# Output projection: the last four rows of every head loaded by four DMA engines, the other rows by sixteen

## The chip, the cores and the metric

One core of one Trainium2 chip runs the program. The metric is the time on the device in microseconds. The profile has its own measure, the span from the first to the last instruction; the time is 1.7 to 2.1 us longer than the span, and that difference will matter.

## The reference, cut to what matters

```python
g = sigmoid((x * gate_w).sum(-1))
q = (x @ wq) as 32 heads of 128              # x is one row of 576
a = softmax(q k^T / sqrt(128)) v, last 4096 keys, 16 kv heads
a = concat(heads) @ wo                       # wo: 4096 x 576, row 128*h + d
b = gelu(x @ w1 + b1) @ w2 + b2              # 576 -> 4608 -> 576
out = g * a + (1 - g) * b
```

All tensors are bf16. With one row of x, every weight and every cached key and value is read once and used once: 53.6 MB in all.

## The kernel before

The large loads are issued in order by SyncE; each covers 128 partitions. The output projection `wo` and the second half of `w2` are the last five of them. The weights `wo` lie as 32 consecutive rows per partition, so partition 4h+a holds rows 32a to 32a+31 of head h. The attention output is spread over partitions in the same way by one small product (`om` with `lo32b`), and every row then costs two products into `y_ps`.

```python
    # ... loads of w1, wq, K; scores; softmax ...
    v_t = [load("v_t", "CD"[g], A_v_cache, g) for g in range(2)]
    nc.sync.dma_start(out=w2_t[:, 0:NJ, :], in_=w2_src[:, 0])
    v_t.append(load("v_t", "A", A_v_cache, 2))
    # ...
    v_t.append(load("v_t", "C", A_v_cache, 3))
    # ...
    RO = Hq * Dh // P                                   # 32
    wo_src = A_wo.rearrange("(p r) n -> p r n", r=RO)
    for r0, r1 in ((0, 16), (16, RO)):
        nc.sync.dma_start(out=wo_t[:, r0:r1, :], in_=wo_src[:, r0:r1, :])
    for j0, j1 in ((0, 10), (10, 16), (16, 18)):
        nc.sync.dma_start(out=w2_t[:, NJ + j0 : NJ + j1, :], in_=w2_src[:, 1, j0:j1, :])
    # om = attention output x (g / sum), one column block per stripe a
    ov_mm = nc.tensor.matmul(ov_ps[:], lhsT=om..., rhs=lo32b[:], start=True, stop=True)
    nc.vector.tensor_copy(out=ov[:], in_=ov_ps[:])
    late = [(gt, f, w2_t[:, f, :]) for f in range(6, NJ)]
    # ... then wo rows and w2 rows in order of arrival; each one two matmuls into y_ps
```

Of the kernel before, what the change touches and what calls it, by code (L numbers as in the profile page):

```python
# [9 lines left out]
FP32 = mybir.dt.float32  # L10
BF16 = mybir.dt.bfloat16
I32 = mybir.dt.int32
ACT = mybir.ActivationFunctionType
ALU = mybir.AluOpType
# [4 lines left out]
def kernel(  # L19
# [15 lines left out]
    nc = tc.nc  # L35

    P = 128
    D = 576
    Hq, Hkv, Dh = 32, 16, 128
# [10 lines left out]
    NI = 2 * D // P  # L50
# [15 lines left out]
        main.instructions.insert(at, first)  # L66

    nc.at_finalize(first_load_ahead)

    def keep_weights(nc):  # L70
        body = nc.main_func.blocks[1]
        loaded, kept = None, []
        for i in body.instructions:
            if type(i).__name__ == "InstLdweights":
                w = i.ins[0]
                key = (w.memref, w.offset, tuple(w.ap), i.tile_size, i.tile_position)
                sync = i.sync_info
                free = sync is None or not (sync.on_wait or sync.on_update)
                if key == loaded and free:
                    continue  # L80
                loaded = key
            elif type(i).__name__ == "InstMatmult" and i.ldweights is not False:
                loaded = None
            kept.append(i)
        body.instructions = kept
# [58 lines left out]
    const = ctx.enter_context(tc.tile_pool(name="const", bufs=1))  # L144
# [4 lines left out]
    ps_m = ctx.enter_context(tc.tile_pool(name="ps_m", bufs=2, space=bass.MemoryType.PSUM))  # L149
# [24 lines left out]

    one_b = const.tile([1, 2], BF16, name="one_b")
    nc.gpsimd.memset(one_b[:], 1.0)
    NCC = 2 * NI + 32 + 4 + 16 + P
    low = const.tile([P, NCC], I32, name="low")
    mask = const.tile([P, NCC], I32, name="mask")
    c0 = 0  # L180
    for base, pattern, keep in (
        (0, [[1, NI], [1, 2]], 1),
        (128, [[-1, 32]], 31),
        (128, [[-32, 4]], 96),
        (128, [[-8, 16]], 120),
        (128, [[-1, P]], 7),
    ):
        n = 1
        for step, num in pattern:
            n *= num  # L190
        nc.gpsimd.iota(low[:, c0 : c0 + n], pattern=pattern, base=base, channel_multiplier=1)
        nc.gpsimd.memset(mask[:, c0 : c0 + n], keep)
        c0 += n
    nc.vector.tensor_tensor(out=low[:], in0=low[:], in1=mask[:], op=ALU.bitwise_and)
    is0 = const.tile([P, NCC], FP32, name="is0")
    nc.gpsimd.tensor_scalar(
        out=is0[:], in0=low[:], scalar1=0.0, scalar2=None, op0=ALU.is_equal
    )
    alt = is0[:, 0 : 2 * NI].rearrange("p (i t) -> p i t", t=2)
    lo32 = is0[:, 2 * NI : 2 * NI + 32]  # L200
    hi4 = is0[:, 2 * NI + 32 : 2 * NI + 36]
    ones = const.tile([P, P], FP32, name="ones")
    nc.gpsimd.memset(ones[:], 1.0)
    ident = const.tile([P, P], BF16, name="ident")
# [4 lines left out]
        out=perm[:],  # L209
        in_=perm[:],  # L210
        pattern=[[-64, 2], [-1, 2], [0, 4], [-2, 32]],
        compare_op=ALU.not_equal,
        fill=1.0,
        base=0,
        channel_multiplier=1,
    )
    lo32b = const.tile([P, 32], BF16, name="lo32b")
    nc.gpsimd.tensor_copy(out=lo32b[:], in_=lo32)
    c0 = 2 * NI + 36
    hi16 = const.tile([P, 16], FP32, name="hi16")  # L220
    nc.gpsimd.tensor_scalar(
        out=hi16[:], in0=is0[:, c0 : c0 + 16], scalar1=-SCALE, scalar2=None, op0=ALU.mult
    )
    same8 = is0[:, c0 + 16 : NCC]
    row_of = const.tile([HB, 16, HB, 2], BF16, name="row_of")
    nc.gpsimd.memset(row_of[:], 0.0)
    nc.gpsimd.affine_select(
        out=row_of[:],
        in_=row_of[:],
        pattern=[[0, 16], [-1, HB], [0, 2]],  # L230
        compare_op=ALU.not_equal,
        fill=1.0,
        base=0,
        channel_multiplier=1,
# [4 lines left out]
        out=foreign[:],  # L239
        in_=foreign[:],  # L240
        pattern=[[0, P], [-1, HB]],
        compare_op=ALU.not_equal,
        fill=0.0,
        base=0,
        channel_multiplier=1,
# [4 lines left out]
        out=xdup.rearrange("p (d t) -> p d t", t=2),  # L250
        in_=x_row.rearrange("p (d o) -> p d o", o=1).to_broadcast([1, D, 2]),
    )
    xs_ps = ps_m.tile([P, NI, 1], FP32, name="xs_ps", tag="m")
    for i in range(NI):
        nc.tensor.matmul(  # L255
            xs_ps[:, i, :],
            lhsT=xdup[:, i : 2 * D : NI],
            rhs=one_b[0:1, 0:1],
            start=(i == 0),
            stop=(i == NI - 1),  # L260
# [4 lines left out]
        out=x2[:], in0=xs_ps[:].to_broadcast([P, NI, 2]), in1=alt, op=ALU.mult  # L265
# [5 lines left out]
        out=junk_row,  # L271
        in0=x_row,
        in1=gw_row,
        scale=1.0,
        scalar=0.0,
        op0=ALU.mult,
# [8 lines left out]
    g_t = const.tile([P, 1], FP32, name="g_t")  # L285
# [3 lines left out]
        out=omg[:], in0=g_t[:], scalar1=-1.0, scalar2=1.0, op0=ALU.mult, op1=ALU.add  # L289
# [2 lines left out]
    nc.vector.tensor_scalar(  # L292
        out=b2g[:], in0=b2_row, scalar1=omg[0:1, 0:1], scalar2=None, op0=ALU.mult
    )
    gh = const.tile([P, 1, 4], FP32, name="gh")
    nc.vector.tensor_scalar(
        out=gh[:, 0, :], in0=hi4, scalar1=g_t[:, 0:1], scalar2=None, op0=ALU.mult
    )


# [19 lines left out]
    for j in range(NJ):  # L320
        nc.tensor.matmul(
            h_ps[:, j:NF:NJ],
            lhsT=b1_t[:, j:FH:NJ],
            rhs=ident[0:2, 0:2],
            start=(j == 0),
            stop=False,
# [5 lines left out]
    for i in range(NI):  # L332
        for j in range(NJ):
            nc.tensor.matmul(  # L334
                h_ps[:, j:NF:NJ],
                lhsT=w1_t[:, i, j:FH:NJ],
                rhs=x2[:, i, :],
                start=False,
                stop=(i == NI - 1 and j == NJ - 1),
# [9 lines left out]
        out=poly[:],  # L349
        in0=z2[:],  # L350
        scalar1=2.0 * C0 * 0.044715,
        scalar2=2.0 * C0,
        op0=ALU.mult,
# [11 lines left out]
        out=gt[:], in0=hacc[:], scalar=omg[:, 0:1], in1=r_t[:], op0=ALU.mult, op1=ALU.mult  # L365
# [4 lines left out]
    for i in range(NI):  # L370
        for j in range(Hq // 2):
            nc.tensor.matmul(  # L372
                q_ps[:, j : Hq : Hq // 2],
                lhsT=wq_t[:, i, j * Dh : (j + 1) * Dh],
                rhs=x2[:, i, :],
                start=(i == 0 and j == 0),
                stop=(i == NI - 1 and j == Hq // 2 - 1),
# [5 lines left out]
    for j in range(4):  # L383
        nc.tensor.matmul(
            qj_ps[:, j, :, :].rearrange("p g q -> p (g q)"),
            lhsT=perm[:, j, :, :].rearrange("p b l -> p (b l)"),
            rhs=q_b[:],
            start=True,
            stop=True,
        )  # L390
    for b in range(4):
# [6 lines left out]
            out=diag[:, :, :, 0:8],  # L398
            in_=qj_ps[quad].rearrange("p j g q -> p g j q"),
# [17 lines left out]
    def queue(engine, emit):  # L417
        if engine in issued:
            with tc.issue_after(issued[engine].ins):
                issued[engine] = emit()  # L420
        else:
            issued[engine] = emit()

    def load(name, tag, cache, g):
        tile_ = big.tile([P, NCK, Dh], BF16, name=name, tag=tag)
        src = cache[0, HB * g : HB * g + HB, Sk - W : Sk, :].rearrange(
            "b (k c) d -> k b (c d)", k=NKP
        )
        nc.sync.dma_start(out=tile_[:].rearrange("p c d -> p (c d)"), in_=src)
        return tile_  # L430
# [105 lines left out]
    v_t = [load("v_t", "CD"[g], A_v_cache, g) for g in range(2)]  # L536
    nc.sync.dma_start(out=w2_t[:, 0:NJ, :], in_=w2_src[:, 0])
    v_t.append(load("v_t", "A", A_v_cache, 2))
    o_ps = ps_m.tile([P, Hq, 1], FP32, name="o_ps", tag="m")

    def value_products(g):
        for c in range(NCK):
# [16 lines left out]
        out=ls[:],  # L559
        in0=same8[:, 0:8].rearrange("p (o q) -> p o q", o=1).to_broadcast([P, NG, 8]),  # L560
        in1=sums[:].to_broadcast([P, NG, 8]),
        op=ALU.mult,
# [6 lines left out]
            t_ps, lhsT=ones[:], rhs=ls[:].rearrange("p g q -> p (g q)"), start=True, stop=True  # L569
        ),  # L570
    )
    rg = const.tile([P, Hq, 1], FP32, name="rg")
# [2 lines left out]
    nc.vector.tensor_tensor(  # L575
        out=rgh[:],
        in0=rg[:].to_broadcast([P, Hq, 4]),
        in1=gh[:].to_broadcast([P, Hq, 4]),
        op=ALU.mult,
    )  # L580
    queue("pe", lambda: value_products(3))


    RO = Hq * Dh // P
    wo_t = big.tile([P, RO, D], BF16, name="wo_t", tag="D")
    wo_src = A_wo.rearrange("(p r) n -> p r n", r=RO)
    for r0, r1 in ((0, 16), (16, RO)):
        nc.sync.dma_start(out=wo_t[:, r0:r1, :], in_=wo_src[:, r0:r1, :])  # L588
    for j0, j1 in ((0, 10), (10, 16), (16, 18)):
        nc.sync.dma_start(out=w2_t[:, NJ + j0 : NJ + j1, :], in_=w2_src[:, 1, j0:j1, :])  # L590

    om = const.tile([P, Hq, 4], BF16, name="om")
    nc.vector.tensor_tensor(  # L593
        out=om[:], in0=o_ps[:].to_broadcast([P, Hq, 4]), in1=rgh[:], op=ALU.mult
    )
    with tc.issue_after(issued["pe"].ins):
        for f in range(6):
            y_add(gt[:, f : f + 1], w2_t[:, f, :])
    ov_ps = ps_m.tile([P, RO], FP32, name="ov_ps", tag="m")
    ov_mm = nc.tensor.matmul(  # L600
        ov_ps[:], lhsT=om[:].rearrange("p h a -> p (h a)"), rhs=lo32b[:], start=True, stop=True
    )
    ov = const.tile([P, RO], BF16, name="ov")
    nc.vector.tensor_copy(out=ov[:], in_=ov_ps[:])

    late = [(gt, f, w2_t[:, f, :]) for f in range(6, NJ)]
    wo_at = [(ov, r, wo_t[:, r, :]) for r in range(RO)]
    w2_at = [(gt, f, w2_t[:, f, :]) for f in range(NJ, NF)]
    late += wo_at[0:8] + wo_at[16:RO] + wo_at[8:13] + w2_at[0:10] + wo_at[13:16] + w2_at[10:]
    before = ov_mm  # L610
    for n, (vec, at, row) in enumerate(late):
# [37 lines left out]
```

## Time and profile before

| | before |
|---|---|
| time, median of 6 runs | 132.50 us (132.35 to 132.66) |
| span of the profiled run | 130.7 us |
| loads' queue, share of 16 DMA engines | 96.4% |
| TensorE busy | 61% |

The main lines of the page stand in the prediction. How to read them: the share of the loads' queue says that the DMA engines are busy nearly all the time, so the kernel is bound by moving bytes, and a product counts only where a landing waits for it. The last pieces of the chain that ended last, in order of time (start, duration, what), show it again:

```profile
93.23 34.61 DMA w_t<-in_B_w_dram
127.84 0.04 issue
127.89 1.19 PE y_ps L306 x16
129.07 0.43 DVE out_row L617
```

The load named here is issued at 93 us and lands at 127.84; for 34.61 us it only stands behind others. What follows its landing takes 1.6 us plus the store.

One thing is not on the page: a load is done when the slowest of its sixteen engines is. The trace stores sixteen increments of the load's semaphore, one for each of the sixteen chains of packets that the prediction describes, and the load counts as landed with the last. For the last piece of w2 in the kernel before, in us of the span:

```
126.66 126.67 126.88 126.90 126.99 127.04 127.07 127.09
128.13 128.20 128.29 128.33 128.35 128.43 128.49 128.58
```

Eight engines finish before the other eight, on average by 1.44 us.

### The profile page before, as it was taken

Reading aid. Unit: us, or ns where it says so; the run is one execution under the profiler, and the core shown is the slowest. Engines: PE = TensorE matmul, PEld = TensorE weight load, DVE = VectorE, ACT = ScalarE, POOL = GpSimd, SP = SyncE. Lnnn points to the kernel's source line nnn. Section 1 sums busy time; section 2 is a strip of 40 time slices with the busy share of each in tenths; the row PEclk is TensorE's granted clock in tenths of the full one; section 3 lists DMA queues with packets and bytes.
Section 4 is the critical chain, followed back from the end, with each engine's and each line's share of the span. In section 5 each row is a group of like instructions: output and inputs, shape, how many; then the busy total and the mean of one; then the engine's idle time right before and its main releaser. Section 6 shows DMA issues by size and latency. Waiting matters only on the chain.

```text
span 130.7 us, 2382 instructions
## 1 busy us (share of the span) xinstructions
PE 79.9 (61%) x1138; PEld 46.0 (35%) x1071; DVE 51.9 (40%) x47; ACT 8.1 (6%) x17; POOL 8.2 (6%) x28
## 2 busy tenths in 40 slices
PE   0037999466002998859909986987100930999573
PEld 0037949366000121211201121677000920945441
DVE  0053000400069969999999995604000010010001
ACT  3000000002100000030003003020000000000001
POOL 6029600000000000000000000000000000000000
PEclk9999999999999999999995999965555555556999
DMA  7999999899899999999999999999989999999980
GB/s 220 431 442 423 474 422 474 372 451 466 381 426 471 401 411 471 411 411 471 421 411 451 441 401 441 413 417 458 456 381 441 461 386 407 434 422 422 398 330 24
DMA packets 2468, 53.75 MB, mean 411 GB/s; under 512 B 278, under 2 KB 282, under 8 KB 540
## 3 DMA queue, kind: packets, MB, share of 16 engines
q1 hardware_dynamic: 2450, 53.61, 96.4%
q8 instruction: 8, 0.13, 0.4%
q10 hardware_dynamic: 10, 0.01, 0.0%
HBM read 53.62 MB, written 0.00 MB: 410 GB/s over the span
## 4 chain that ended last, share of the span: by engine, by line
DMA 54%; DVE 24%; PE 13%; issue 6%; SPq 1%; DVEq 0%
DMA k_t<-in_A_k_cache_dram 27%; DMA w_t<-in_B_w_dram 26%; DVE kt L441 19%; PE s_ps L463 7%; PE o_ps L543 5%; DVE m L479 3%; DVE pt L512 2%; PE y_ps L306 1%; SPq L588 1%; DVE mr L482 1%; PE mt_ps L488 0%; DVE out_row L617 0%; SPq L172 0%; SPq L590 0%; SPq L168 0%
## 5 line engine op out<-in xcount | busy, mean ns | idle before, releaser
L463 PE MATMUL s_ps<-kt,qz_flat 128*128 128x512 bf16 x128 | 32.3, 409 | 17.3 <-DVE kt L441 10.4
L441 DVE STREAM_TRANSPOSE kt<-k_t 128x4096 f32<-128x4096 f32 x8 | 35.3, 4432 | 11.8 <-DMA k_t<-in_A_k_cache_dram 10.7
L543 PE MATMUL o_ps<-pt,v_t 128*128 128x8 bf16 x512 | 14.2, 167 | 16.7 <-DMA v_t<-in_A_v_cache_dram 15.4
L463 PEld LDWEIGHTS <-qz_flat 128*128 128x128 bf16 x64 | 6.8, 106 | 40.1 <-issue 40.0
L543 PEld LDWEIGHTS <-v_t 128*128 128x128 bf16 x512 | 14.1, 103 | 17.5 <-DMA v_t<-in_A_v_cache_dram 15.6
L334 PE MATMUL h_ps<-x,w_t 128*128 128x2 bf16 x162 | 10.4, 202 | 0.0
L334 PEld LDWEIGHTS <-w_t 128*128 128x128 bf16 x162 | 10.2, 162 | 0.5 <-issue 0.4
L306 PE MATMUL y_ps<-w_t,gt 128*1 128x288 bf16 x72 | 7.4, 361 | 1.1 <-DMA w_t<-in_B_w_dram 1.1
L500 ACT ACTIVATE p_t<-s_ps,negm 128x1024 bf16<-128x1024 f32 x4 | 4.5, 1114 | 50.6 <-DVE negm L496 50.6
L573 DVE RECIPROCAL rg<-mt_ps 128x32 f32<-128x32 f32 x1 | 0.4, 358 | 15.8 <-PE mt_ps L568 15.8
L512 DVE STREAM_TRANSPOSE pt<-p_t 128x1024 bf16<-128x1024 bf16 x4 | 4.9, 1224 | 2.7 <-ACT p_t L500 2.7
L372 PE MATMUL q_ps<-x,wq_t 128*128 128x2 bf16 x144 | 4.0, 166 | 3.1 <-DMA wq_t<-in_A_wq_dram 3.1
L306 PE MATMUL y_ps<-wo_t,ov 128*1 128x288 bf16 x64 | 4.9, 299 | 1.4 <-DMA wo_t<-in_A_wo_dram 1.4
L343 DVE COPY hacc<-h_ps 128x36 f32<-128x36 f32 x1 | 0.2, 196 | 13.2 <-PE h_ps L334 13.2
L617 DVE CAST out_row<-y_ps 1x288 bf16<-1x288 f32 x1 | 0.4, 445 | 12.3 <-PE y_ps L306 12.3
L479 DVE TENSOR_REDUCE m<-s_ps 128x1 f32<-128x1024 f32 x4 | 4.8, 1196 | 1.1 <-PE s_ps L463 1.1
L255 PE MATMUL xs_ps<-one_b,rows 1*128 1x1 bf16 x9 | 0.7, 196 | 7.2 <-DVE rows L249 7.2
L372 PEld LDWEIGHTS <-wq_t 128*128 128x128 bf16 x144 | 3.9, 104 | 3.2 <-DMA wq_t<-in_A_wq_dram 3.2
L306 PEld LDWEIGHTS <-gt 128*1 128x1 bf16 x72 | 3.6, 97 | 3.8 <-issue 1.9
L306 PEld LDWEIGHTS <-ov 128*1 128x1 bf16 x64 | 3.1, 90 | 2.9 <-issue 1.7
L593 DVE TENSOR_TENSOR om<-o_ps,rgh 128x128 bf16<-128x128 f32 x1 | 0.3, 291 | 8.6 <-PE o_ps L543 8.6
L249 DVE COPY rows<-rows 1x1152 bf16<-1x1152 bf16 x1 | 0.7, 748 | 6.4 <-DMA rows<-in_A_x_dram 6.4
(64 smaller groups left out, 33.5 us busy)
## 6 DMA issues: line engine op xcount, KB each, us to landing
k_t<-in_A_k_cache_dram SPq DMA_DIRECT2D x4, 4096.0 KB, 33.8
v_t<-in_A_v_cache_dram SPq DMA_DIRECT2D x4, 4096.0 KB, 23.3
wq_t<-in_A_wq_dram SPq DMA_DIRECT2D x1, 4608.0 KB, 26.1
wo_t<-in_A_wo_dram SPq DMA_DIRECT2D x2, 2304.0 KB, 30.0
w_t<-in_B_w_dram SPq DMA_DIRECT2D x1, 2880.0 KB
w_t<-in_B_w_dram SPq DMA_DIRECT2D x1, 2592.0 KB
w_t<-in_B_w_dram SPq DMA_DIRECT2D x1, 2304.0 KB, 8.0
w_t<-in_B_w_dram SPq DMA_DIRECT2D x1, 1440.0 KB
```

The lines of the kernel that those rows point to most:

```text
L249: nc.vector.tensor_copy(out=xdup.rearrange("p (d t) -> p d t", t=2), in_=x_row.rearrange("p (d o) -> p d o", o=1).to_broadcast([1, D, 2]),)
L306: last = nc.tensor.matmul(y_out[s], lhsT=vec, rhs=row[:, s * DH : (s + 1) * DH], start=start, stop=stop, skip_group_check=True,)
L334: nc.tensor.matmul(h_ps[:, j:NF:NJ], lhsT=w1_t[:, i, j:FH:NJ], rhs=x2[:, i, :], start=False, stop=(i == NI - 1 and j == NJ - 1), skip_grou ...
L372: nc.tensor.matmul(q_ps[:, j : Hq : Hq // 2], lhsT=wq_t[:, i, j * Dh : (j + 1) * Dh], rhs=x2[:, i, :], start=(i == 0 and j == 0), stop=(i ...
L441: lambda: nc.vector.transpose(out=kt[g, f][:].bitcast(FP32), in_=keys.rearrange("p c d -> p (c d)").bitcast(FP32),),
L463: last = nc.tensor.matmul(s_ps[g][:, u * 512 : (u + 1) * 512].rearrange("p (c k) -> p c k", k=32), lhsT=qz(g, j, 2 * f + half), rhs=kv[:, ...
L479: queue("dve", lambda: nc.vector.reduce_max(out=m1[:], in_=s_ps[g][:], axis=AX.X))
L482: lambda: nc.vector.tensor_scalar(out=mr[:], in0=hi16[:], scalar1=m1[:, 0:1], scalar2=None, op0=ALU.mult),
L500: nc.scalar.activation(out=p_t[:].rearrange("p c k -> p (c k)"), in_=s_ps[g][:], func=ACT.Exp, bias=negm[:, 0:1], scale=SCALE, accum_out=s ...
L512: lambda: nc.vector.transpose(out=pt[:, g, :, :].rearrange("p c q -> p (c q)"), in_=p_t[:].rearrange("p c k -> p (c k)"),),
L543: last = nc.tensor.matmul(o_ps[:, 8 * g : 8 * g + 8, 0], lhsT=v_t[g][:, c, :], rhs=pt[:, g, c % 32, 8 * (c // 32) : 8 * (c // 32) + 8], st ...
L588: nc.sync.dma_start(out=wo_t[:, r0:r1, :], in_=wo_src[:, r0:r1, :])
```

## The change

The intent is to give more bytes to DMA engines that finish early. Of every head, rows 124 to 127 are taken out of the even split and loaded by two DMAs whose access pattern is rewritten to an outermost dimension of four, so that they run on four engines. The trace does not number the engines. The other 124 rows go as four stripes of 31 over all sixteen. The core of the diff:

```diff
+    def split_outer(nc):      # for the two tail loads only
+                    ins=[copy.replace(src, ap=[[4 * step, 4], [step, 4], [1, size]])],
+                    outs=[copy.replace(dst, ap=[[part, 16], [1, 1], [1, size]])],
 ...
+    RW = 31
 ...
+    om_t = const.tile([P, 64], BF16, name="om_t")
+    wo_tail = const.tile([48, 4, D], BF16, name="wo_tail")
 ...
     v_t.append(load("v_t", "A", A_v_cache, 2))
+    for u in range(2):
+        load_tail = nc.sync.dma_start(
+            out=wo_tail[32 * u : 32 * u + 16].rearrange("h j n -> h (j n)"),
+            in_=wo_src[16 * u : 16 * u + 16, 4 * RW : P, :].rearrange("h j n -> h (j n)"),
+        )
 ...
-    RO = Hq * Dh // P
+    RO = RW
 ...
+    nc.vector.tensor_scalar(out=rgt[:], in0=rg[:, :, 0], scalar1=gh[:, 0, 4:5], ...)
+    nc.vector.tensor_tensor(out=om_t..., in0=o_ps..., in1=rgt..., op=ALU.mult)
+        ov_mm = nc.tensor.matmul(
+            ov_ps[0:64, RO : RO + 4], lhsT=om_t[:], rhs=lo31[:, 0:4], start=True, stop=True
+        )
+    nc.scalar.copy(out=ov_tail[:], in_=ov_ps[0:48, RO : RO + 4])
 ...
+    late += [(ov_tail, j, wo_tail[:, j, :]) for j in range(4)]
```

The masks that select a stripe's rows are rebuilt on GpSimd for stripes of 31 instead of 32.

More of the change, by code (lines that the diff above doesn't have):

```diff
@@ L68 @@
     nc.at_finalize(first_load_ahead)
+    four_engines = []
+    def split_outer(nc):
+        body = nc.main_func.blocks[1]
+        kept = []
+        for i in body.instructions:
+            if i.name in four_engines:
+                src, dst = i.ins[0], i.outs[0]
+                (step, n), (one, size) = src.ap
+                part = dst.ap[0][0]
+                assert n == dst.ap[0][1] == 16 and one == 1
+                i = copy.replace(
+                    i,
+                    ins=[copy.replace(src, ap=[[4 * step, 4], [step, 4], [1, size]])],
+                    outs=[copy.replace(dst, ap=[[part, 16], [1, 1], [1, size]])],
+                    ant_dge_precooked=False,
+                )
+            kept.append(i)
+        body.instructions = kept
+    nc.at_finalize(split_outer)
     def keep_weights(nc):
@@ L176 @@
     nc.gpsimd.memset(one_b[:], 1.0)
-    NCC = 2 * NI + 32 + 4 + 16 + P
+    NCC = 2 * NI + 16 + P
     low = const.tile([P, NCC], I32, name="low")
@@ L182 @@
         (0, [[1, NI], [1, 2]], 1),
-        (128, [[-1, 32]], 31),
-        (128, [[-32, 4]], 96),
         (128, [[-8, 16]], 120),
@@ L199 @@
     alt = is0[:, 0 : 2 * NI].rearrange("p (i t) -> p i t", t=2)
-    lo32 = is0[:, 2 * NI : 2 * NI + 32]
-    hi4 = is0[:, 2 * NI + 32 : 2 * NI + 36]
     ones = const.tile([P, P], FP32, name="ones")
@@ L216 @@
     )
-    lo32b = const.tile([P, 32], BF16, name="lo32b")
-    nc.gpsimd.tensor_copy(out=lo32b[:], in_=lo32)
-    c0 = 2 * NI + 36
+    RW = 31
+    hi5 = const.tile([P, 5], FP32, name="hi5")
+    nc.gpsimd.memset(hi5[:], 1.0)
+    nc.gpsimd.affine_select(
+        out=hi5[:],
+        in_=hi5[:],
+        pattern=[[-RW, 5]],
+        compare_op=ALU.is_ge,
+        fill=0.0,
+        base=0,
+        channel_multiplier=1,
+    )
+    nc.gpsimd.affine_select(
+        out=hi5[:],
+        in_=hi5[:],
+        pattern=[[RW, 5]],
+        compare_op=ALU.is_ge,
+        fill=0.0,
+        base=RW - 1,
+        channel_multiplier=-1,
+    )
+    lo31 = const.tile([P, RW], BF16, name="lo31")
+    nc.gpsimd.memset(lo31[:], 0.0)
+    for a in range(5):
+        nc.gpsimd.affine_select(
+            out=lo31[:],
+            in_=lo31[:],
+            pattern=[[-1, RW]],
+            compare_op=ALU.not_equal,
+            fill=1.0,
+            base=-RW * a,
+            channel_multiplier=1,
+        )
+    om_t = const.tile([P, 64], BF16, name="om_t")
+    nc.gpsimd.memset(om_t[:], 0.0)
+    wo_tail = const.tile([48, 4, D], BF16, name="wo_tail")
+    nc.gpsimd.memset(wo_tail[:].bitcast(FP32), 0.0)
+    c0 = 2 * NI
     hi16 = const.tile([P, 16], FP32, name="hi16")
@@ L294 @@
     )
-    gh = const.tile([P, 1, 4], FP32, name="gh")
+    gh = const.tile([P, 1, 5], FP32, name="gh")
     nc.vector.tensor_scalar(
-        out=gh[:, 0, :], in0=hi4, scalar1=g_t[:, 0:1], scalar2=None, op0=ALU.mult
+        out=gh[:, 0, :], in0=hi5[:], scalar1=g_t[:, 0:1], scalar2=None, op0=ALU.mult
     )
@@ L538 @@
     v_t.append(load("v_t", "A", A_v_cache, 2))
+    wo_src = A_wo.rearrange("(h d) n -> h d n", d=P)
+    for u in range(2):
+        load_tail = nc.sync.dma_start(
+            out=wo_tail[32 * u : 32 * u + 16].rearrange("h j n -> h (j n)"),
+            in_=wo_src[16 * u : 16 * u + 16, 4 * RW : P, :].rearrange("h j n -> h (j n)"),
+        )
+        four_engines.append(load_tail.ins.name)
     o_ps = ps_m.tile([P, Hq, 1], FP32, name="o_ps", tag="m")
@@ L577 @@
         in0=rg[:].to_broadcast([P, Hq, 4]),
-        in1=gh[:].to_broadcast([P, Hq, 4]),
+        in1=gh[:, :, 0:4].to_broadcast([P, Hq, 4]),
         op=ALU.mult,
     )
+    rgt = const.tile([P, Hq], FP32, name="rgt")
+    nc.vector.tensor_scalar(
+        out=rgt[:], in0=rg[:, :, 0], scalar1=gh[:, 0, 4:5], scalar2=None, op0=ALU.mult
+    )
     queue("pe", lambda: value_products(3))
-    RO = Hq * Dh // P
+    RO = RW
     wo_t = big.tile([P, RO, D], BF16, name="wo_t", tag="D")
-    wo_src = A_wo.rearrange("(p r) n -> p r n", r=RO)
     for r0, r1 in ((0, 16), (16, RO)):
-        nc.sync.dma_start(out=wo_t[:, r0:r1, :], in_=wo_src[:, r0:r1, :])
+        nc.sync.dma_start(
+            out=wo_t[:, r0:r1, :].rearrange("p r n -> p (r n)"),
+            in_=wo_src[:, 0 : 4 * RW, :].rearrange("h (a r) n -> h a (r n)", a=4)[
+                :, :, r0 * D : r1 * D
+            ],
+        )
     for j0, j1 in ((0, 10), (10, 16), (16, 18)):
@@ L598 @@
             y_add(gt[:, f : f + 1], w2_t[:, f, :])
-    ov_ps = ps_m.tile([P, RO], FP32, name="ov_ps", tag="m")
-    ov_mm = nc.tensor.matmul(
-        ov_ps[:], lhsT=om[:].rearrange("p h a -> p (h a)"), rhs=lo32b[:], start=True, stop=True
-    )
+    nc.vector.tensor_tensor(
+        out=om_t[:].rearrange("p (u h) -> p u h", u=2)[:, :, 0:16],
+        in0=o_ps[:, :, 0].rearrange("p (u h) -> p u h", u=2),
+        in1=rgt[:].rearrange("p (u h) -> p u h", u=2),
+        op=ALU.mult,
+    )
+    ov_ps = ps_m.tile([P, RO + 4], FP32, name="ov_ps", tag="m")
+    ov_mm = nc.tensor.matmul(
+        ov_ps[:, 0:RO],
+        lhsT=om[:].rearrange("p h a -> p (h a)"),
+        rhs=lo31[:],
+        start=True,
+        stop=True,
+    )
+    with tc.issue_after(ov_mm.ins):
+        ov_mm = nc.tensor.matmul(
+            ov_ps[0:64, RO : RO + 4], lhsT=om_t[:], rhs=lo31[:, 0:4], start=True, stop=True
+        )
     ov = const.tile([P, RO], BF16, name="ov")
-    nc.vector.tensor_copy(out=ov[:], in_=ov_ps[:])
+    nc.vector.tensor_copy(out=ov[:], in_=ov_ps[:, 0:RO])
+    ov_tail = const.tile([48, 4], BF16, name="ov_tail")
+    nc.scalar.copy(out=ov_tail[:], in_=ov_ps[0:48, RO : RO + 4])
     late = [(gt, f, w2_t[:, f, :]) for f in range(6, NJ)]
```

## The prediction

What no trace or run here shows is cut out of the recorded texts, and the cuts are marked. Cut from this one: how a load's access pattern decides the number and the choice of its engines, how instructions are brought in, and what an unaligned run costs. The sum as recorded came to -0.25 to -0.34 us, from 132.52 to about 132.2; its term of up to 0.1 us for unaligned stripes is cut, so only -0.34 is left.

Engine numbers in the recorded texts are names: 0 to 3 for the four engines that bring the tails, in t4k8 and t8k8 0 to 7 for the eight that do, and 4 to 7 for the eight without the first four. That there would be four was the assumption. "I can place only two of the four" means the two chains of the b1 load: that they are two of the four was assumed too.

> **What bounds the kernel now.** I read the page first, then the windows by stage, the chain in order of time, the timeline of the last 20 us, and last the single DMA packets and semaphore landings stored in the trace. From the page:
>
> ```profile
> span 130.7 us, 2382 instructions
> PE 79.9 (61%) x1138; PEld 46.0 (35%) x1071; DVE 51.9 (40%) x47; ACT 8.1 (6%) x17; POOL 8.2 (6%) x28
> ...
> DMA  7999999899899999999999999999989999999980
> ...
> q1 hardware_dynamic: 2450, 53.61, 96.4%
> q8 instruction: 8, 0.13, 0.4%
> ...
> DMA 54%; DVE 24%; PE 13%; issue 6%; SPq 1%; DVEq 0%
> ```
>
> No compute engine is above 61%, while the loads' queue alone keeps all sixteen DMA engines busy for 96.4% of the span, with no idle slice before the last one. The kernel is a stream of 53.6 MB. The chain names compute as well, but a compute stage costs time only if the stream stops for it, and it doesn't. The windows, with DMA share and GB/s as last columns, say the same by stage:
>
> ```profile
> 50.00:90.00 40.00, 31.03 (x303) 11.48 (x251) 33.71 (x23) 4.82 (x8) 0.00 (x0) 0.91 1.00 431
> 90.00:112.00 22.00, 6.64 (x227) 6.42 (x224) 0.65 (x2) 0.00 (x0) 0.00 (x0) 0.50 0.99 422
> 112.00:122.00 10.00, 8.94 (x161) 5.89 (x158) 0.48 (x2) 0.00 (x0) 0.00 (x0) 0.60 0.99 416
> ```
>
> The timeline of the end shows what TensorE waits for:
>
> ```profile
> 122.29 2.74 PE L306 MATMUL y_ps<-wo_t,ov 128*1 128x288 bf16 x42 [1.35 <-DMA wo_t<-in_A_wo_dram]
> ...
> 125.77 1.39 PE L306 MATMUL y_ps<-w_t,gt 128*1 128x288 bf16 x20 [0.74 <-DMA w_t<-in_B_w_dram]
> ...
> 127.89 1.15 PE L306 MATMUL y_ps<-w_t,gt 128*1 128x288 bf16 x16 [0.36 <-DMA w_t<-in_B_w_dram]
> ...
> 129.06 0.45 DVE L617 CAST out_row<-y_ps 1x288 bf16<-1x288 f32 x1 [12.30 <-PE y_ps L306]
> ```
>
> The idle time in brackets ends at a landing each time. The end is the landing of the next-to-last piece of w2 (127.84), sixteen matmuls, a cast and the store; the last piece lands at 128.58, just in time for its four.
>
> **Inside the sixteen engines.** A load is complete only when its slowest engine is. The packet records carry no engine number, but give start, duration and size: each 128-partition load is 128 packets, eight per engine, and a packet follows its predecessor within a few ns (mostly an overlap of 3), so they can be joined into sixteen chains of 153 packets. The result is clean. Eight chains end at 126.19 to 126.65 us, eight at 127.63 to 128.13. Each late chain has exactly one hole of 1.00 to 1.08 us with a packet about 0.5 us too long behind it, some 1.5 us in all. The holes coincide with the eight packets of the instruction queue (16384 B, 1.01 to 1.10 us, the first at 18.5, the last at 121.7). Each instruction fetch thus costs one engine about 1.5 us, and the eight fetches hit eight different engines. The landings agree: the sixteen increments of the last w2 piece fall at 126.66 to 127.09 (eight) and 128.13 to 128.58 (eight). Half of the engines are idle for the last 1.4 us.
>
> [...]the two-partition b1 load shows as two packets of 4608 B on two different chains; neither, nor the chain with the one-partition rows, has a hole.[...]
>
> **The change part by part.**
>
> Loads. The output projection stays 4.72 MB. Per head, rows 0 to 123 go as four stripes of 31 rows over 128 partitions, rows 124 to 127 as two loads of sixteen 4608 B runs. The first wo load keeps 18432 B per partition, the second shrinks to 15 rows, 17280 B. An 18432 B packet takes 0.686 us undisturbed, so the shrunk one about 0.643: eight per engine save 0.343 us on every engine. Engines 0 to 3 each receive eight packets of 4608 B at 178 ns (the duration of b1's) and two semaphore packets of 9 ns: 1.44 us more, net +1.10. Late engines: 127.63-128.13 minus 0.34 is 127.29-127.79. Engines 0 to 3, if early: 126.19-126.65 plus 1.10 is 127.29-127.75. The two meet: the sizes look chosen for that gap. The last landings come 0.34 us sooner. Nothing smaller in bytes moves; this is balance, and its limit is the 1.4 us gap spread over all, 0.7 us.
>
> Alignment. A stripe starts at a multiple of 31x1152 = 35712 B, which is 128 past a multiple of 256 for the second and fourth stripe of a head.[...]
>
> Issue. The two tail loads stand between the third and fourth load of V. The third is issued at 79.66, the fourth at 86.56 behind a wait for TensorE; two issues at about 0.5 us each (the V issues take 0.54) fit there. Semaphores move on by two: the last two w2 loads now wait for older loads (first w2 half, third V load) to land, at 91.8 and 101.5 by the landings, over 20 us before their data is due. Free.
>
> TensorE. One more small product for the tail vector (about 0.2), eight tail matmuls of 0.10 to 0.14 (24 gt matmuls took 3.26, 16 wo matmuls 1.64), two fewer wo matmuls later. In front of the 122.29 wait it has 1.35 us idle and needs 1.0 to 1.3 more; the landing comes 0.34 earlier, so it may arrive 0 to 0.3 late there, and the 0.74 of idle time before the next landing absorbs that. Nothing on the path.
>
> VectorE and ScalarE. One 128x32 scale, one 128x32 product (0.15 to 0.3 each, by their neighbours) and a 48x4 copy. The product comes before the copy of ov, but TensorE has twelve matmuls (1.6 us) to do meanwhile. GpSimd. Six rows more, about 2 us of memsets and selects; its last memset ends at 15.14 now, and its first user is the ScalarE copy at 31.97. Free.
>
> Sum: -0.34[...], from 132.52 to about 132.2.
>
> **The rivals.** First, engines 2 or 3 (or all four, should the assignment of fetches change from run to run) are late ones. Then an engine ends at up to 128.13 + 1.10 = 129.2 and the time is 133.6. For it: I can place only two of the four. Against: eight distinct engines in eight fetches looks like a fixed order, and the three timed runs lie within 0.18 us. Second, the unaligned stripes run slower[...]: if 5%, eight packets of 0.69 lose 0.28 us per engine and the gain is gone, 132.5; if 30%, 134. Third, TensorE becomes the bound before the second wo part at its halved clock (0.60 in that window) and carries the delay through to the end: it would have to lose 1.1 us more than its idle time; at most +0.3. Fourth, the tails are spread over sixteen engines after all: everything stays as even as now, 132.5.
>
> **Range and chances.** Weights of roughly 70% for the balance as designed (132.1 to 132.3), 15% for no net effect (132.4 to 132.6), 15% for a late engine among the four or slow stripes (132.8 to 133.7). The centre is 132.2, the range 132.0 to 132.9. Two per cent would be 2.65 us; only very slow stripes reach that upwards, and nothing reaches it downwards, the whole imbalance being worth 0.7.
>
> **What would show it.** Right: the second wo load's packets are 17280 B at about 0.643 us, 32 packets of 4608 B at 0.178 sit on four chains, those four end within 0.2 us of the late eight, and the landing before the last matmuls comes at about 127.5. Wrong: a landing of the last loads with one to four increments about 1 us behind all others (a loaded late engine); wo packets from odd stripes visibly longer; an idle time of zero before the last w2 matmuls (TensorE the bound); 4608 B packets on sixteen chains. GB/s over the span should go up by 0.3% at most.

## The result

| | before | changed |
|---|---|---|
| time, median of 6 runs | 132.50 us | 132.38 us (132.26 to 132.57) |
| span of the profiled run | 130.7 us | 130.3 us |
| last increment of the last w2 load | 128.58 | 128.07 |

The ratio is 0.9991, with a 95% interval from 0.9978 to 1.0004. A ratio is the mean time of one kernel's fast runs over that of the other's fast runs of the same rounds, so it is not quite the ratio of the medians. The prediction was 132.2, with a range of 132.0 to 132.9: right. But the time moved by 0.12 us where some 0.3 was stated, this result alone does not separate it from no change, and the range also held the prediction's own case of no net effect (132.4 to 132.6). The span of the profiled run moved by 0.4 us. Where the rest went is one question for the experiments.

The page of the changed kernel, the same lines as in the prediction:

```profile
span 130.3 us, 2411 instructions
PE 80.7 (62%) x1145; PEld 46.1 (35%) x1077; DVE 53.7 (41%) x49; ACT 8.3 (6%) x18; POOL 10.1 (8%) x34
...
q1 hardware_dynamic: 2490, 53.61, 96.5%
q8 instruction: 8, 0.13, 0.4%
...
DMA 52%; DVE 24%; PE 14%; issue 6%; SPq 2%
```

Same bytes, forty packets more (32 of tail data and 8 for semaphores), the same eight instruction fetches, 29 instructions more. The timeline of the end of the changed kernel:

```profile
116.60 3.04 PE L359 MATMUL y_ps<-w_t,gt 128*1 128x288 bf16 x24
...
119.57 1.05 PE L359 MATMUL y_ps<-wo_tail,ov_tail 48*1 48x288 bf16 x8
...
121.89 2.61 PE L359 MATMUL y_ps<-wo_t,ov 128*1 128x288 bf16 x40 [0.19 <-DMA wo_t<-in_A_wo_dram]
...
125.35 1.39 PE L359 MATMUL y_ps<-w_t,gt 128*1 128x288 bf16 x20 [0.85 <-DMA w_t<-in_B_w_dram]
...
127.44 1.15 PE L359 MATMUL y_ps<-w_t,gt 128*1 128x288 bf16 x16 [0.33 <-DMA w_t<-in_B_w_dram]
```

The eight tail products took 1.05 us and used up the idle time in front of the second wo load: 1.35 us before, 0.19 now. But the bracket is still there, so a landing and not TensorE starts the 121.89 group, and this and the two later groups that waited start 0.4 us sooner than before. The chain ends accordingly:

```profile
94.31 33.08 DMA w_t<-in_B_w_dram
127.39 0.04 issue
127.44 1.19 PE y_ps L359 x16
128.62 0.43 DVE out_row L702
```

And the sixteen increments of the last w2 piece:

```
125.92 126.26 126.48 126.55
127.38 127.62 127.69 127.70 127.73 127.74 127.76 127.76 127.84 127.85 128.02 128.07
```

Joined into chains, the packets show who is who. The four chains with 4608 B packets have no hole, and their last packets end at 126.93 to 127.59. The eight chains with a hole end at 127.18 to 127.44. Four chains with neither end at 125.43 to 126.11. So the two loaded groups meet, as designed, and the last packet of all (127.59) is now one of a tail engine.

### The profile page after: what moved, and what is told of

Its sections match the earlier page's. It is cut to its first block, busy times and chain, and to the rows that moved or that the text cites. A ratio compares the mean times of both kernels' runs of the same rounds, so it can differ in the third digit from the quotient of the medians.

```text
span 130.3 us, 2411 instructions
## 1 busy us (share of the span) xinstructions
PE 80.7 (62%) x1145; PEld 46.1 (35%) x1077; DVE 53.7 (41%) x49; ACT 8.3 (6%) x18; POOL 10.1 (8%) x34
## 3 DMA queue, kind: packets, MB, share of 16 engines
q1 hardware_dynamic: 2490, 53.61, 96.5%
## 4 chain that ended last, share of the span: by engine, by line
DMA 52%; DVE 24%; PE 14%; issue 6%; SPq 2%
DMA k_t<-in_A_k_cache_dram 27%; DMA w_t<-in_B_w_dram 25%; DVE kt L494 19%; PE s_ps L516 7%; PE o_ps L603 5%; DVE m L532 3%; DVE pt L565 2%; PE y_ps L359 1%; SPq L651 1%; DVE mr L535 1%; SPq L658 0%; SPq L194 0%; PE mt_ps L541 0%; DVE out_row L702 0%; SPq L190 0%
## 5 line engine op out<-in xcount | busy, mean ns | idle before, releaser
L359 PE MATMUL y_ps<-wo_t,ov 128*1 128x288 bf16 x62 | 4.3, 286 | 0.2 <-DMA wo_t<-in_A_wo_dram 0.2
L359 PEld LDWEIGHTS <-ov 128*1 128x1 bf16 x62 | 2.6, 83 | 1.8 <-issue 0.8
```

Source lines behind the costliest of these rows:

```text
L359: last = nc.tensor.matmul(y_out[s], lhsT=vec, rhs=row[:, s * DH : (s + 1) * DH], start=start, stop=stop, skip_group_check=True,)
```

## The experiments

All outputs are right. I give the time, the mean span of the timed runs, and the time less the span ("outside"). The spans are recorded to 0.1 us.

| version | fast runs | time (mean) | span (mean) | outside | 8192 B fetch after the end |
|---|---|---|---|---|---|
| before, beside the first four | 11 | 132.45 | 130.71 | 1.74 | no |
| a_again: changed kernel | 5 | 132.37 | 130.42 | 1.95 | yes |
| t4k16: tails on 16 engines | 5 | 133.93 | 131.96 | 1.97 | yes |
| t4k8: tails on eight engines | 5 | 132.64 | 130.76 | 1.88 | yes |
| t8k8: eight rows on eight engines | 6 | 133.36 | 131.45 | 1.91 | yes |
| before, beside the next four | 7 | 132.43 | 130.69 | 1.75 | no |
| b_pool6: before, 6 GpSimd more | 4 | 132.39 | 130.65 | 1.74 | no |
| b_dve2_act1: before, 2 VectorE, 1 ScalarE more | 4 | 132.51 | 130.60 | 1.91 | yes |
| fetch9: before, 256 TensorE more | 4 | 133.74 | 131.98 | 1.77 | no |
| t4spread: 16 engines, spread partitions | 4 | 132.94 | 130.85 | 2.09 | yes |
| before, beside the next three | 9 | 132.46 | 130.70 | 1.76 | no |
| merged | 5 | 132.10 | 130.10 | 2.00 | yes |
| a_third: changed kernel | 5 | 132.15 | 130.20 | 1.95 | yes |
| b_act1: before, 1 ScalarE, 1 GpSimd more | 4 | 132.42 | 130.65 | 1.77 | no |
| before, beside the last | 7 | 132.44 | 130.67 | 1.77 | no |
| b_sp2: before, 2 small loads more | 4 | 132.39 | 130.68 | 1.71 | no |

The last column is read in the profiled run of each version.

### a_again and a_third: the changed kernel again, on two chips

No edit. Expected:

> The changed kernel once more, for a tighter interval. Balance theory (the end follows the slowest of sixteen DMA engines; the change takes 0.34 us of data from the eight engines that fetch instructions and gives engines 0 to 3, which fetch none, 1.10 us): ratio about 0.9975, 0.3 us less than the kernel before; the four chains with 4608 B packets have no hole and end within 0.3 us of the eight chains with a hole. Rival A (the balance is worth nothing by the clock, the trace's 0.4 us is a run's chance): ratio 0.999 to 1.001.

> The changed kernel beside the merged one on the same chip: span 130.4, time less span 1.95, 132.35 us, ratio 0.999 to 0.9995; the late fetch is there.

Measured: ratio 0.9995 (0.9983 to 1.0007) on one chip and 0.9979 (0.9965 to 0.9993) on another; by the table, 0.08 and 0.31 us less time, 0.29 and 0.50 us less span. Both ratios missed what I had written: the first lies in the rival's range, the second below the 0.999 that I then expected. The trace of the first repeat has four chains of tail packets without a hole ending at 127.22 to 127.60, as in the first trace. The gain in the span was there both times: the longest span of the changed kernel (130.5 and 130.4) is below the shortest of the kernel before in the same rounds (130.6). The gain in the time was within the noise once and clear of it once, and both times the part outside the span had grown by 0.2 us. So rival A, "a run's chance", fell for the span; for the time the first repeat alone would not have refuted it.

The trace of the first repeat shows one thing more:

```profile
121.29 4.25 PE L359 MATMUL y_ps<-wo_t,ov 128*1 128x288 bf16 x56
125.38 1.39 PE L359 MATMUL y_ps<-w_t,gt 128*1 128x288 bf16 x20
...
127.47 1.14 PE L359 MATMUL y_ps<-w_t,gt 128*1 128x288 bf16 x16 [0.33 <-DMA w_t<-in_B_w_dram]
```

The first two groups have no wait in front. The granted clock was 0.50 from 116 to 122 us here and 0.63 in the first trace. TensorE came to the second wo load at 122.93, 1.35 us after its landing (121.58), and had made up for it only before the last group.

### t4k16: the same layout, tails on sixteen engines

```diff
-    nc.at_finalize(split_outer)
```

> The changed kernel without the rewriting of the two tail loads, so that each of the sixteen engines brings one 4608 B row per load; layout, products and TensorE work as in the changed kernel. Balance theory: every engine loses 0.343 us and gets 2 x 178 + 18 ns back, so the late engines end where they did before the change; the time is that of the kernel before (ratio 0.999 to 1.001), some 0.3 us above the changed kernel. Rival A: the same time as the changed kernel. Rival B[...]: the sixteen engines write partitions 0-15 and 32-47 at once and hinder each other; 4608 B packets take well over 178 ns, 300 or more.

Measured: 134.02 us, ratio 1.0111 (1.0093 to 1.013). This was the surprise. Neither balance (132.5) nor rival A foresaw it; rival B, by which the partitions written count, foresaw the slow packets (300 ns or more), without a size for the time. The durations of the 4608 B packets fit B: 178 to 534 ns, a tenth of them over 505 ns, against 178 to 185 in the changed kernel. Thirty packets of 32768 B, of the V loads around them, took 1.6 to 2.2 us instead of 1.21, and one that followed an instruction fetch 2.6. All increments of the last piece came late, the early eight at 128.03 to 128.65, the others at 129.38 to 129.85: the whole stream was held up, not one engine. TensorE was not the cause; its last group still waits:

```profile
127.11 1.39 PE L358 MATMUL y_ps<-w_t,gt 128*1 128x288 bf16 x20 [0.85 <-DMA w_t<-in_B_w_dram]
...
129.18 1.14 PE L358 MATMUL y_ps<-w_t,gt 128*1 128x288 bf16 x16 [0.32 <-DMA w_t<-in_B_w_dram]
```

So the sixteen engines hindered each other. Why they do so in partitions 0-15 and 32-47 no trace shows. That the partitions are what counts is tested by t4spread, below. In the changed kernel four engines write the same 32 partitions, and no tail packet is slowed (178 to 185 ns). So the choice of partitions and the choice of four engines belong together.

### t4spread: sixteen engines, partitions spread

```diff
-    nc.at_finalize(split_outer)
-            out=wo_tail[32 * u : 32 * u + 16]...
+            out=wo_tail[64 * u : 64 * u + 64 : 4]...       # 0, 4, .. 60 and 64, 68, .. 124
```

> The tails of four rows once more on all sixteen engines, one row each per load, but written to partitions 0, 4, .. 60 by the first load and 64, 68, .. 124 by the second, where the version that took 134.0 us wrote partitions 0-15 and 32-47. [...]4608 B packets of 178 to 370 ns instead of up to 534, no 32768 B packet drawn out to 2.1 us but some by 0.2, and a span of 130.9 to 131.2. Rival (any tail on sixteen engines costs 1.3 us, by its small packets): span 132.0 again.

Measured: 132.94 us, ratio 1.0038 (1.0023 to 1.0053); span 130.85. The 4608 B packets took 178 to 293 ns, and forty of the 32768 B packets beside them took 1.24 to 1.43 us instead of 1.21, as the expectation had it. Sixteen engines with the same 32 small packets cost 0.16 us of span here and 1.25 us there, against the kernel before: the partitions decide. How, it does not show. The span came out 0.05 below the range I had given. The increments of the last piece are again eight early (126.66 to 127.35) and eight late (128.34 to 128.69), as in the kernel before: an even split keeps the imbalance. With the changed kernel's layout and as much work on TensorE, but no load on four engines, the gain in the span is gone.

### t4k8 and t8k8: eight engines

One tail load on partitions 0-31 with an outermost dimension of eight, meant to run on eight engines, four rows each. It does in t8k8: the page has 40 packets more in the loads' queue than before (2490 and 2450), 32 of data and eight of semaphores. Which eight they are no trace shows.

```diff
-                    ins=[... ap=[[4 * step, 4], [step, 4], [1, size]]],
-                    outs=[... ap=[[part, 16], [1, 1], [1, size]]],
+                    ins=[... ap=[[4 * step, 8], [step, 4], [1, size]]],
+                    outs=[... ap=[[part, 32], [1, 1], [1, size]]],
```

t8k8 also has `RW = 30`, eight tail rows of each head, two scratch tiles moved to make room, and the products of twelve w2 rows moved ahead of the last value products.

> The same four rows of a head, but as one load on 32 partitions[...]. Balance theory, if the eight engines that fetch no instructions are 0 to 7: eight chains with 4608 B packets, none with a hole, ending at 126.2 to 126.6 + 0.39, under the late ones; late engines as in the changed kernel; the time is that of the changed kernel or up to 0.15 us less. If engines 4 to 7 fetch instructions: four chains with both a hole and 4608 B packets, ending 0.39 us later than in the kernel before: ratio 1.003.

> Eight rows of a head[...], stripes of 30 rows; the first 12 w2 products moved ahead of the last value products so that TensorE has room for the tail's sixteen matmuls. Balance theory, if engines 0 to 7 fetch nothing: late engines lose 0.686 us, engines 0 to 7 gain 4 x 0.35 - 0.686 = +0.71; both end at about 127.2 to 127.4; 0.6 to 0.7 us less than the kernel before, ratio 0.995, and 0.3 less than the changed kernel. If engines 4 to 7 fetch: 0.7 us more than the kernel before. Rival A: no difference from the kernel before. Rival C (TensorE's tail work eats the gain): idle time zero before the last w2 products and a time above that of the changed kernel.

Measured: 132.60 us, ratio 1.0016 (1.0004 to 1.0028), and 133.25 us, ratio 1.007 (1.005 to 1.009). Both came out on the side where some of the eight fetch instructions; in the second the 0.74 us of span are what that branch said (0.7). The increments of its last piece are the clearest reading. From the kernel before, with 0.686 taken from every engine and 1.40 added to the eight that bring the tail, one expects four levels: 125.97-126.40 for an engine with neither tail nor fetch, 127.37-127.80 with the tail only, 127.44-127.89 with a fetch only, 128.84-129.29 with both. Measured:

```
126.26 126.26
127.22 127.32 127.33 127.42 127.45 127.48 127.50 127.55 127.56 127.60 127.65 127.71
128.93 129.17
```

Two, twelve, two. So of the eight engines with a tail two fetch, and of the other eight six do. The four of the changed kernel are free, or its own increments would show it (the last is at 128.07); so the two are not of those four, if the fetches fall on the same engines in every run, which was not shown. In t4k8 two increments stand alone at 128.47 and 128.57, the rest end at 127.94, which agrees: I had written four such engines there and it was two. TensorE did not limit t8k8:

```profile
122.90 3.71 PE L358 MATMUL y_ps<-wo_t,ov 128*1 128x288 bf16 x38 [0.41 <-DMA wo_t<-in_A_wo_dram]
...
128.50 1.14 PE L358 MATMUL y_ps<-w_t,gt 128*1 128x288 bf16 x16 [0.29 <-DMA w_t<-in_B_w_dram]
```

It waits for a landing there too, so rival C is out. The w2 group between these two had no idle time in front: there TensorE was late, but it caught up before the last group. What the moved products are worth was not tested.

### fetch9: 256 TensorE instructions more

```diff
+    junk = ps_s.tile([P, 1024], FP32, name="junk", tag="s")
+    queue("pe", more_instructions)     # 128 value products of V load 2 again, into junk
     queue("pe", lambda: value_products(3))
```

> The kernel before with 128 more weight loads and products on TensorE, into a dead PSUM tile, in the 5.7 us in which it waits for the last V load (they take 3.6 us). That is 256 instructions[...]. Theory of fetches: nine 16384 B packets of the instruction queue instead of eight, nine holes of 1.0 to 1.1 us. If the ninth falls on an engine that had none, seven early and nine late engines and the time of the kernel before; if on one that had one already[...], one increment of the last loads some 1.45 us behind the others and 1.4 us more, ratio 1.011. Rival (the hole is something of time, not of instructions): eight fetches and holes as before.

Measured: 133.71 us, ratio 1.0098 (1.0078 to 1.0118). The queues of this kernel:

```profile
q1 hardware_dynamic: 2450, 53.61, 95.3%
q8 instruction: 9, 0.15, 0.5%
```

Nine fetches for 256 more instructions. The last piece's increments are eight at 126.50 to 127.13, seven at 128.16 to 128.37, and one at 129.87. The ninth fetch fell on an engine that already had one, and cost it another 1.5 us; the program ended 1.3 us later. The added products themselves did not do it, since the last two w2 groups still wait for landings:

```profile
127.06 1.39 PE L306 MATMUL y_ps<-w_t,gt 128*1 128x288 bf16 x20 [1.03 <-DMA w_t<-in_B_w_dram]
...
129.18 1.15 PE L306 MATMUL y_ps<-w_t,gt 128*1 128x288 bf16 x16 [0.36 <-DMA w_t<-in_B_w_dram]
```

So the hole follows from the instructions and not from the time, and one 16384 B fetch on the wrong engine (1.29 us of span) costs some three to four times what this change gains there (0.29 and 0.50). It also fits a fixed order of engines, but one run does not prove one: the ninth hole lies on the chain of the first fetch or on that of the sixth, which run within 1 ns of each other.

### b_pool6, b_dve2_act1, b_act1, b_sp2: what grew outside the span

The changed kernel's trace holds one 8192 B packet of the instruction kind 1.75 us after its last instruction; the kernel before has none. Each of these four adds to the kernel before only instructions whose result nobody uses, on one or two engines (b_act1 has one GpSimd memset besides):

```diff
+    for n in range(6): nc.gpsimd.memset(idle[:, n : n + 1], 0.0)      # b_pool6
+    for n in range(2): nc.vector.memset(idle[:, n : n + 1], 0.0)      # b_dve2_act1
+    nc.scalar.copy(out=idle[:, 2:3], in_=idle[:, 0:1])                # b_dve2_act1, b_act1
+    nc.sync.dma_start(out=idle[:, u, :], in_=gate_w...)               # b_sp2, u = 0, 1
```

Theory E was that the six GpSimd instructions bring the late packet, or in b_dve2_act1 the VectorE and ScalarE ones, and that otherwise all stays as in the kernel before; b_act1 asks which of those two does, b_sp2 whether two more DMAs on SyncE do.

> The kernel before with six more one-column memsets on GpSimd at about 2 us, where it idles. The changed kernel has six more GpSimd instructions than the kernel before; its span fell by 0.29 us in five rounds but its time by only 0.08, and its trace holds one 8192 B fetch some 1.75 us after the last instruction that the kernel before lacks. Theory E[...]: the span stays at 130.7, the late fetch appears, and time less span rises from 1.74 to about 1.95 us.[...]

> The kernel before with two more VectorE memsets and one more ScalarE copy of one column each, at the start where both wait. As many as the changed kernel adds. Theory E for these engines: late 8192 B fetch and time less span about 1.95 us, span 130.7. Otherwise as the kernel before, 1.74.

> The kernel before with one more one-column ScalarE copy (and one GpSimd memset, shown harmless). [...]if ScalarE's, the late 8192 B fetch appears and time less span is about 1.91; if VectorE's, neither, 1.74.

> The kernel before with two more loads on SyncE (1152 B each, into a tile nobody reads) at the place of the changed kernel's tail loads; like those they also make the last two w2 loads wait for older loads. The merged version kept the late 8192 B fetch with no more VectorE and ScalarE instructions than the kernel before, so: [...]the late fetch is there and time less span is about 1.93; if not, 1.75 and something else in the merged version is the cause. The span stays at 130.7[...].

Measured: only b_dve2_act1 has the late packet (512 ns), and only its outside part rose, from 1.75 to 1.91 us. One ScalarE instruction alone does not do it, so the VectorE instructions do. The time ratios (0.9997, 1.0006, 0.9999, 0.9997) are too coarse for 0.17 us: it is the time less the span that shows it. In the table, the eight rows with the late packet have 1.88 to 2.09 us outside, the eight without it 1.71 to 1.77. That the packet delays the end is inferred from this order; no run shows what waits for it.

With its semaphore and drain instructions, which the page does not count as busy, VectorE has 58 instructions in the trace of each version without the late packet (before, b_pool6, b_act1, b_sp2, fetch9), and 59 or 60 in each trace with it (60 in b_dve2_act1 and t4spread, 59 in all others). No other engine's count separates the two groups. So the late packet goes with VectorE's stream, and one instruction more may be enough; only two more were tested alone.

### merged: the same loads with no more VectorE and ScalarE instructions

The edit, abridged to one line a part:

```diff
-    rgt = ...; separate scale product                 # now a fifth column of rgh
-    nc.vector.tensor_scalar(out=gh...)                # now on GpSimd
-    nc.scalar.copy(out=ov_tail[:], in_=ov_ps[0:48, RO : RO + 4])
+    tail products accumulate into ov_ps[:, RO : RO + 4]; one VectorE copy of [P, RO + 4]
```

> The changed kernel's loads, with the vectors of the projection made by as many VectorE and ScalarE instructions as the kernel before has (47 and 13): the two scale products are one, one small product moved to GpSimd, the tail of ov accumulates into the same PSUM tile and one copy takes both. Balance plus fetch theory: span 130.4 as in the changed kernel, no 8192 B fetch after the end, time less span 1.74; 132.15 us, ratio 0.9975 to 0.998 to the kernel before, clear of 1. Rival (the late fetch is not what costs 0.2 us outside the span, or the two more SyncE instructions cause it): time less span stays at 1.9 and the time at 132.35.

Measured: 132.12 us, ratio 0.9975 (0.9962 to 0.9987), the best of all versions beside the changed kernel on the same chip (0.9979), but not separable from it. The reason I gave for it failed: the late packet is there, and 2.00 us lie outside. The span is 130.10 against 130.20. So the instructions counted in the program are not the whole story. SyncE was my next suspect, and b_sp2 cleared it in the kernel before. The trace has the likely answer: VectorE's 47 busy instructions are those of the kernel before, but ten semaphore instructions stand beside them in place of nine, which makes 59. No run was made with that one instruction taken out, so this is a match of counts and not a test.

## Why the prediction was right

- **The bound.** Right. The last group of products waits for a landing, for 0.29 to 0.36 us, in every trace shown. Earlier groups do not always (a_again, t8k8).
- **The imbalance and its cause.** Right, and now shown: a ninth fetch made a ninth delay of 1.5 us (fetch9).
- **The terms of the loads.** The smaller wo packets took 0.644 us (0.643 predicted), the tail packets 178 to 185 ns (178), and the unaligned stripes cost nothing that shows in the mean: the 18432 B packets of the first wo load, half of them unaligned, have a mean of 0.690 us; those of wo before have 0.691, without one that a fetch had drawn out. The second rival is out, and the up to 0.1 us that the sum had left for alignment wasn't needed.
- **Which engines.** Right, but I placed only two of the four, and those by an assumption; that all four are early was a bet that came off. All four tail chains are free of holes in both traces looked at (the first and a_again), and t8k8 counts two fetching engines among its eight with a tail and six among the others. The first rival is out.
- **The path of TensorE.** Right at the end, narrowly on the way. In the first trace the tail products took 1.05 us, and of 1.35 us of idle time before the second wo load 0.19 were left. In the first repeat, at a granted clock of 0.50, TensorE was 1.35 us late there, where I had allowed 0.3, and the idle time before the next landing was used up too. The third rival's first half came true in that trace; its second half, the delay at the end, did not, since the last group still waited 0.33 us.
- **The fourth rival's size was wrong.** I wrote that sixteen engines would leave all as it was, 132.5. It is 134.0 (t4k16), since I counted engines and forgot the partitions that they write. It doesn't touch the forecast, because the change doesn't do that.
- **The sum.** "-0.25 to -0.34 us" is the span's: it fell by 0.29 and 0.50 in the repeats. As a sum for the time it lacked a term: +0.2 us outside the span, which goes with VectorE's stream being one instruction longer and shows as one late 8 KiB fetch. I had called the additional vector work free because it is off the path inside the span. That was true, and not enough. A second, smaller thing was not foreseen: an engine's 64 packets of 32768 B add up to 77.94 to 77.97 us in the three traces of the changed kernel and to 78.04 before, up to 0.1 us less. Why is open.

## What to carry to other kernels

When a kernel is bound by its DMA stream (the loads' queue at 96.4% here), look at the sixteen increments of the last load: if they fall into two groups (1.44 us apart here), bytes can move from the slow engines to the fast ones, at best for half the gap (an estimate for groups of equal size, 0.7 us here; 0.29 and 0.50 us of span were gained). Find out first which engines are fast: moved to eight engines of which two were slow, such bytes cost time (ratio 1.0016 in t4k8, 1.007 in t8k8). Try other partitions too: two small loads on sixteen engines held up the whole stream when they wrote partitions 0-15 and 32-47 (t4k16, 1.25 us of span; 134.02 us, and 132.34 with four engines in the same rounds), and cost 0.16 us when they wrote every fourth partition (t4spread). Count instructions as bytes of the stream: 256 more on TensorE brought one more 16384 B fetch and cost 1.29 us of span in fetch9, with the loads' queue at 95.3%.
